# Sketched attention with a routed expert layer: two changes of order, the count of the first half moved ahead of its take, and a search and pick moved behind a copy

## The chip, the cores and the metric

The kernel runs on one core of a Trainium2 chip. A core has five engines that run side by side[...]: TensorE (PE, with its weight loads shown apart as PEld), VectorE (DVE), ScalarE (ACT), GpSimd (POOL) and SyncE (SP), which here issues most of the transfers. The metric is the device time of one execution in microseconds; less is better.

## What is computed

The first half is attention with a polynomial sketch, for q, k and v of 4 batches, 4 heads, 1088 rows and 32 columns. Its result, seen as 4352 rows (tokens) of 128, goes to a layer of 8 experts, of which each token uses one.

```python
def phi(x):                                   # 8 by 8 products of two sketches
    a = einsum('rd,bhsd->bhsr', S1, x); b = einsum('rd,bhsd->bhsr', S2, x)
    return einsum('bhsi,bhsj->bhsij', a, b).reshape(..., 64)
q_p, k_p = phi(q), phi(k)
kv, z = einsum('bhsf,bhsd->bhfd', k_p, v), k_p.sum(axis=2)
attn = einsum('bhsf,bhfd->bhsd', q_p, kv) / (einsum('bhsf,bhf->bhs', q_p, z)[..., None] + 1e-6)
x = attn.transpose(0, 2, 1, 3).reshape(4352, 128)

xn = x / (norm(x) + 1e-6); en = emb / (norm(emb) + 1e-6)
logits = xn @ en.T / tau
expert_idx = argmax(logits, axis=1)
probs = softmax(logits); gate_w = probs[arange(N), expert_idx]
for e in range(8):
    mask = expert_idx == e
    out[mask] = gate_w[mask, None] * (relu(x[mask] @ w1[e]) @ w2[e])
```

## The kernel before, in words

**Two halves of the tokens.** The four batches are worked in two halves (m = 0 and 1), each of two batches. For a half, the keys' features are made and multiplied with v (L479), and the queries' features give the numerators and denominators in PSUM (`nd`, L613). `x` (L626 to L633, on DVE) divides them and makes the rows `xg` and the scaled logits `lg`.

**The router.** For a stretch of columns of a half, `router` (L677) makes these steps. `best` (L683, L684) searches the largest logit and stores the distances into the row. `pick` (L690 to L695) makes the one-hot choice `oh` and its sum `total`. `place` (L703 to L707) adds up on TensorE, in PSUM, each token's place within its expert. `take` (L712, DVE) reads those sums out of PSUM with the one-hot choice, and `split` (L718 to L720) and `mark` (L727) prepare a product that inverts the list. `write` (L733, L737) sends the rows to DRAM through SP. Half 0 is one stretch; half 1 has two, columns 0 to 7 and 8 to 16.

**The count.** `count` in `plan_early` (L831) calls `tokens_by_expert` (L820): two small products on TensorE (L824, over `less` and the first half's `total`) and one rounding on DVE (L825), which gives the number of full blocks of each expert. The count of half 0 lies in the same PSUM tile as the placing (`spare[0]`), in other columns. `rest` (L835 to L839), `find` (L791, L795), `sums` (L800, L802) and `tokens` (L817) turn counts and places into the lists of rows of the first ten blocks, which the gathers (`fetch`, L930, on POOL) use.

**The blocks.** Tokens of one expert are gathered in blocks of 128 rows, counted from 0. For block i: `turn` (L936 on TensorE, and the copy L938, on ACT for blocks 0, 1 and 4 to 8, else on DVE), `up` (first layer, L984, and the rectifier L992 on ACT), `down` (second layer, L1020), and the scaled store (L1029, L1032). The gate needs `norm` (L997, L998), `inverse` (L1001), `shares` (L1008) and `share` (L1011, L1012). `weights` (L947, SP) loads the first layer's weights two blocks ahead.

**What sets the order.** The engines' instructions are in the order in which the steps are emitted. Two lists written by hand, `HEAD` and `ORDER`, hold the steps up to block 0. From then on there are ticks, one for each block (tick 10 is block 0), and within a tick the steps are sorted by a rank: `up` at 30, `turn` of the next block at 45, `share` at 73, `down` of the block before at 74, `norm` at 74.6. Steps of the second half's router are put in by pairs (tick, rank). Each engine takes its part of that order and works it off in sequence.

Of the kernel before, what the change touches and what calls it, by code (L numbers as in the profile page):

```python
# [65 lines left out]
def kernel(  # L66
# [25 lines left out]
    def ps_big():  # L92
        return psum.tile([P, 2, 512], F32, tag="big", bufs=2, name="ps_big")
# [159 lines left out]
    total = {(m, c): consts.tile([P, E], BF16, name=f"total{m}_{c}") for m in range(NM) for c, _ in SPANS[m]}  # L253
# [108 lines left out]
total0; ktr 1; ktr 3; tremb; kab 0 ab; trkv0; kvT0; kb 0; kab 1 acc; kp 0; ktr r; kve0; kz0; kb 1; kab 3 ab;  # L362
ktr 2; nd 0 0; kab 2 t; kab r ab; nd 0 1; x 0 0; kb 2; x 0 1; trqp0r; nd 0 2; kb 3; kp 1; kb r; kv 0; x 0 2;
nd 0 3; kp 2; x 0 3; qtr 1; kp 3; qtr 0; kv 2; qab 0 t; qb 0; qtr 3; kp r; best 0; kv 3; qtr r; qp 0; qtr 2;
place 0; take 0; count; kv 1; kv r; trqp 0; total; split 0; qab 1 t; trkv; qab 3 ab; rest; mark 00; qb 1;
qab r ab; mark 01; find; exp0; kvT; qab 2 acc; sums; kve; qb 2; qpT 0; qb 3; qb r; qp 1; tokens; qp 3; kz;
trqp 1; nd 1 0; fetch0; fetch 1; qp 2; x 1 0; qp r; trqp 3; qpT 1; others; qpT 3; nd 1 1; x 1 1; norm 0; turn 0; trqp 2;
qpT 2
# [154 lines left out]
    def queries(m, c0, c1, tick=None):  # L523
# [128 lines left out]
        if c1 == s1:  # L652

            bank = (lambda: spare[m]) if m == 0 else ps_small if c1 < NC else (lambda: table_bank[0][:, 0])
            best, pick, place, take, split, mark, write = router(m, s0, s1, g, bank)

            if m == 0:
                steps.update({"best 0": best, "pick 0": pick, "place 0": place, "take 0": take, "split 0": split,
                              "mark 00": lambda: mark(0, NK), "mark 01": lambda: mark(NK, NC), "write 0": write})
            elif c1 < NC:  # L660
                at_rank = {best: (10, 72), pick: (10, 72), write: (11, 80), place: (12, 31.5),
                           take: (12, 44), split: (13, 76.5), mark: (14, 76)}
            else:
                at_rank = {best: (12, 31), pick: (12, 31), place: (13, 31), take: (13, 32), split: (13, 32),
                           write: (12, 90), mark: (16, 32)}
                put_at(13)(0, 30.9, lambda: table_bank.append(ps_big()))
            if m == 1:
                for f, (t, rank) in at_rank.items():
                    put_at(t)(0, rank, f)
# [157 lines left out]
    def plan_early():  # L827

        full, upto, w = column("full"), column("upto0"), column("w_early")

        def count():  # L831
            tokens_by_expert((less,), full, spare[0][:, NC * E:(NC + 1) * E])

        def rest():
            nc.vector.tensor_tensor_scan(out=upto[:], data0=ones_e[:], data1=full[:], initial=0.0, op0=ALU.mult, op1=ALU.add)  # L835
            nc.vector.tensor_scalar(w, full, -1.0, float(KEYS), op0=ALU.mult, op1=ALU.add)
            first, early["expert_0"], early["experts"] = blocks(0, upto, w, lane)
            at = first()
            nc.vector.tensor_add(at, at, lane[:, :EARLY])  # L839
            early["key"] = at  # L840

        def others():
            nc.vector.tensor_scalar_min(c_early[:, 1:], upto, float(EARLY))
            early["took"] = column("took")
            nc.vector.tensor_sub(early["took"], c_early[:, 1:], c_early[:, :E])
        return count, rest, others
# [195 lines left out]
    def put_at(tick):  # L1042
        def put(after, rank, f):
            at.setdefault(tick + after, []).append((rank, len(at.get(tick + after, ())), f))
        put.tick = tick
        return put

    for i, group in enumerate(GROUPS):
        for tiles in group:
            for m in range(NM):  # L1050
                keys(m, *tiles, i)
                queries(m, *tiles, i)
# [5 lines left out]
    count, rest, others = plan_early()  # L1058
# [20 lines left out]
    count, rest, shared, others, experts = plan_late()  # L1079
# [100 lines left out]
```

## Time and profile before

| | |
|---|---|
| time, median of 3 runs | 205.55 us (205.15 to 206.97) |
| the profiled execution | 204.43 us |
| its span, first to last instruction | 202.6 us |
| instructions | 6949 |
| TensorE's granted clock | 1.000 |
| HBM read, written | 34.37 MB, 4.73 MB |

The page of the profile begins with busy time by engine and gives the chain of work that ended last. Further views are the waits (who stood still, and what released it), and the timeline: start in us, duration in us, engine, line, operation, `out<-in`, shapes and count, and in brackets the idle time before it with its releaser. A row with x16 is sixteen instructions merged. PE's rows are the products, PEld's the loads of their weights; ends of PE's rows are modelled.

### The profile page before, as it was taken

How to read it: one execution, taken by the hardware profiler on the slowest of the kernel's cores; microseconds unless marked ns; L12 is line 12 of the kernel's file. 1: busy time of each engine (PE TensorE's matmuls, PEld its weight loads, DVE VectorE, ACT ScalarE, POOL GpSimd, SP SyncE). 2: the span in 40 equal slices, each digit the busy share in tenths (PEclk: the TensorE clock that was granted, in tenths of full speed). 3: DMA queues.
4: the chain of work that ended last, by engine and by line, in shares of the span. 5: the costliest groups of instructions: out<-in, count | busy, mean ns of one | idle time of the engine just before them, and what ended most of it. 6: DMA issues, size and time to landing. Idle time of an engine off the chain costs nothing.

```text
span 202.6 us, 6949 instructions
## 1 busy us (share of the span) xinstructions
PE 192.7 (95%) x2586; PEld 182.7 (90%) x2586; DVE 87.6 (43%) x378; ACT 102.4 (51%) x293; POOL 107.0 (53%) x137
## 2 busy tenths in 40 slices
PE   7889999999799999999999999999999999999991
PEld 7667888889689999999999999999999999988991
DVE  6677848888658488912222212222122122112200
ACT  2657451436464456434655546545555465766540
POOL 4000335303813767755878777677676776664043
PEclk9999999999999999999999999999999999999999
DMA  4998799987284886544466665657646784485000
GB/s 132 323 217 287 179 320 293 280 282 208 54 321 139 278 310 211 165 132 145 148 205 189 170 205 155 209 166 163 222 147 184 223 306 169 136 263 190 3 26 25
DMA packets 28162, 39.42 MB, mean 195 GB/s; under 512 B 5738, under 2 KB 21366, under 8 KB 28130
## 3 DMA queue, kind: packets, MB, share of 16 engines
q1 hardware_dynamic: 25776, 34.23, 55.9%
q0 software_dynamic: 2304, 4.74, 7.5%
q8 instruction: 22, 0.36, 0.7%
q14 instruction: 10, 0.08, 0.1%
q10 hardware_dynamic: 50, 0.01, 0.0%
HBM read 34.37 MB, written 4.73 MB: 193 GB/s over the span
## 4 chain that ended last, share of the span: by engine, by line
PE 90%; DVE 4%; ACT 2%; issue 1%; DMA 1%; POOL 0%; POOLq 0%; DVEq 0%
PE ps_big L984 28%; PE ps_ab L1020 14%; PE ps_acc L1020 13%; PE ps_big L613 5%; PE ps_acc L479 4%; PE ps_big L989 4%; PE ps_t L382 3%; PE ps_t L936 2%; PE ps_ab L401 2%; PE ps_big L561 2%; PE ps_acc L1023 2%; PE ps_ab L1023 2%; PE ps_t L802 2%; ACT qpT L570 1%; PE ps_ab L591 1%
## 5 line engine op out<-in xcount | busy, mean ns | idle before, releaser
L984 PE MATMUL ps_big<-xTb,wb 128*128 128x128 f32 x512 | 63.0, 276 | 1.6 <-ACT xTb L938 1.4
L984 PEld LDWEIGHTS ps_big<-xTb,wb 128*128 128x128 f32 x512 | 59.7, 192 | 2.4 <-ACT xTb L938 1.6
L1032 POOL DMA_INDIRECT out_dram<-y,dst_i x36 | 37.7, 1048 | 42.9 <-ACT y L1029 24.4
L992 ACT ACTIVATE hT<-ps_big 128x1024 f32<-128x1024 f32 x36 | 36.9, 1024 | 41.3 <-issue 22.7
L930 POOL DMA_INDIRECT xs<-rows,dst_i x36 | 37.3, 1035 | 18.8 <-DVE dst_i L817 11.3
L938 DVE COPY xTb<-ps_t 128x128 f32<-128x128 f32 x29 | 8.4, 290 | 59.4 <-issue 38.2
L1020 PE MATMUL ps_ab<-w_sb,hT 128*128 x256 | 31.3, 275 | 0.0
L1020 PE MATMUL ps_acc<-w_sb,hT 128*128 x256 | 31.2, 275 | 0.0
L1020 PEld LDWEIGHTS ps_ab<-w_sb,hT 128*128 128x128 f32 x256 | 29.9, 192 | 0.0
L1020 PEld LDWEIGHTS ps_acc<-w_sb,hT 128*128 128x128 f32 x256 | 29.9, 192 | 0.0
L998 POOL TENSOR_TENSOR norm<-norm,half_c 128x1 f32<-128x1 f32 x36 | 21.6, 604 | 4.5 <-ACT sq L997 4.1
L1011 DVE TENSOR_SCALAR gate<-gate 128x1 f32<-128x1 f32 x36 | 5.5, 152 | 23.2 <-ACT probs L1008 16.4
L1029 ACT ACTIVATE y<-ps_ab,gate 128x128 f32<-128x128 f32 x17 | 6.2, 367 | 11.0 <-PE ps_ab L1020 6.4
L1029 ACT ACTIVATE y<-ps_acc,gate 128x128 f32<-128x128 f32 x18 | 6.6, 366 | 9.9 <-PE ps_acc L1020 6.8
L1008 ACT ACTIVATE probs<-xs,norm 128x8 f32<-128x8 f32 x36 | 10.6, 295 | 1.2 <-DVE norm L1001 1.2
L997 ACT ACTIVATE sq<-xs 128x128 f32<-128x128 f32 x36 | 10.8, 301 | 0.2
L936 PE MATMUL ps_t<-ident,xs 128*128 128x128 f32 x36 | 10.2, 282 | 0.2 <-issue 0.2
L417 POOL TENSOR_TENSOR kp<-both 128x1024 f32<-128x1024 f32 (+1 forms) x4 | 6.5, 1624 | 7.0 <-ACT both L412 4.8
L479 PE MATMUL ps_acc<-v,kp 128*64 128x64 f32 x256 | 9.2, 225 | 0.5 <-issue 0.5
L319 POOL TENSOR_TENSOR emb_ss<-emb_ss,half_c 8x1 f32<-8x1 f32 x1 | 0.6, 576 | 17.1 <-ACT emb_sq L318 17.1
L479 PEld LDWEIGHTS ps_acc<-v,kp 128*64 128x64 f32 x256 | 8.2, 138 | 1.5 <-issue 1.5
L989 PE MATMUL ps_big<-xTb,wb 128*64 128x64 f32 x128 | 8.3, 224 | 0.3 <-issue 0.2
(254 smaller groups left out, 293.7 us busy)
## 6 DMA issues: line engine op xcount, KB each, us to landing
wb<-in_moe_w_dram SPq DMA_DIRECT2D x36, 512.0 KB
w_sb<-in_moe_w_dram SPq DMA_DIRECT2D x16, 256.0 KB
rows<-xg SPq DMA_DIRECT2D x4, 544.0 KB
v<-in_v_dram SPq DMA_DIRECT2D x4, 512.0 KB
v<-in_moe_w_dram SPq DMA_DIRECT2D x4, 512.0 KB
k<-in_k_dram SPq DMA_DIRECT2D x3, 512.0 KB
q<-in_q_dram SPq DMA_DIRECT2D x3, 512.0 KB
xs<-rows,dst_i POOLq DMA_INDIRECT x36
```

The costliest lines, as they stand in the source:

```text
L479: nc.tensor.matmul(acc[m][u * HALF:(u + 1) * HALF, i, p], s["kp"][:, c - c0, h], bass.AP(tensor=vo.tensor, offset=vo.offset, ap=[list(vo.a ...
L930: nc.gpsimd.indirect_dma_start(out=xs[i][:], out_offset=None, in_=rows[:2 * S if t == 0 else N + 1], in_offset=bass.IndirectOffsetOnAxis(a ...
L936: nc.tensor.transpose(ps[:, :P], xs[i][:, :DM], ident)
L984: nc.tensor.matmul(ps[:, u, j * P:(j + 1) * P], w[:, f * P:(f + 1) * P], x, start=True, stop=True)
L989: nc.tensor.matmul(ps[r, u, j * P + b * HALF:j * P + (b + 1) * HALF], wh[:, f * P + c * HALF:f * P + (c + 1) * HALF], x[:, b * HALF:(b + 1 ...
L992: nc.scalar.activation(hT[i], ps, ACT.Relu)
L997: nc.scalar.activation(sq, xs[i][:, :DM], ACT.Square, accum_out=norms[i])
L998: nc.gpsimd.tensor_tensor(out=norms[i], in0=norms[i], in1=half_c, op=ALU.pow)
L1008: nc.scalar.activation(p, xs[i][:, DM:], ACT.Exp, scale=norms.pop(i)[:, 0:1], accum_out=gate[i])
L1020: nc.tensor.matmul(ps, h[:, f * P:(f + 1) * P], ws[0][:, f], start=f == 0, stop=f == NF - 1)
L1029: nc.scalar.activation(y, ps, ACT.Copy, scale=gate.pop(i)[:, 0:1])
L1032: d = nc.gpsimd.indirect_dma_start(out=out[:, :], out_offset=bass.IndirectOffsetOnAxis(ap=dst_i[t][:, j:j + 1], axis=0), in_=y[:], in_offs ...
```

## The change

Two places in the order change; no instruction is added, removed or altered in its operands.

In `ORDER`, `count` moves from behind `take 0` to ahead of it. TensorE's order stays as it was, since `take` has no product: the placing, then the count's two products. On DVE the rounding of the count (L825) now comes ahead of the take (L712).

For the first stretch of half 1, `best` and `pick` move from (10, 72) to (11, 45.1) and (11, 45.2). Tick 11 has `turn` of block 2 at rank 45, so they come right behind that block's copy of turned rows. Between the old and the new place on DVE lie `share` of block 0 (L1011, L1012) and the copy of block 2 (L938); these three now run first, and then the six operations of `best` and `pick`. The orders of TensorE, ACT, POOL and SP are the same as before.

```diff
@@ -362,7 +362,7 @@
-place 0; take 0; count; kv 1; kv r; trqp 0; total; split 0; qab 1 t; trkv; qab 3 ab; rest; mark 00; qb 1;
+place 0; count; take 0; kv 1; kv r; trqp 0; total; split 0; qab 1 t; trkv; qab 3 ab; rest; mark 00; qb 1;
@@ -658,7 +658,7 @@
             elif c1 < NC:
-                at_rank = {best: (10, 72), pick: (10, 72), write: (11, 80), place: (12, 31.5),
+                at_rank = {best: (11, 45.1), pick: (11, 45.2), write: (11, 80), place: (12, 31.5),
                            take: (12, 44), split: (13, 76.5), mark: (14, 76)}
```

## The prediction

> **What bounds the kernel now.** I read the share of busy time and the chain that ended last on the page, then TensorE's waits in the stretch of the two edits, then the timeline around each edit.
>
> ```profile
> PE 192.7 (95%) x2586; PEld 182.7 (90%) x2586; DVE 87.6 (43%) x378; ACT 102.4 (51%) x293; POOL 107.0 (53%) x137
> ...
> PE 90%; DVE 4%; ACT 2%; issue 1%; DMA 1%; POOL 0%; POOLq 0%; DVEq 0%
> ```
>
> TensorE is busy 95% of the span and makes 90% of the chain. A change of order on other engines can only win where TensorE stands still. Its waits from 40 to 80 us, complete (sum, times, longest):
>
> ```profile
> PE ps_big L984 <- ACT xTb L938: 1.4, 1, 1.4
> PE ps_big L824 <- DVE lt L712: 0.4, 1, 0.4
> PE ps_big L984 <- DVE norm L1001: 0.2, 1, 0.2
> ```
>
> The second and third are the places that the change touches; the first lies between them and is untouched. From 64.70 on a block takes 3.68 us on TensorE (L1020 starts at 71.32, 75.00, 78.69), with hardly a gap to the end, so what is won before 64.70 should reach the end and nothing more is to be had after it.
>
> First place (timeline: start, duration, engine, line, operation, idle before it and releaser):
>
> ```profile
> 41.46 0.10 PEld L824 LDWEIGHTS <-ones 128*128 128x128 bf16 x1
> 41.66 0.30 DVE L712 TENSOR_TENSOR lt<-ps_big,oh 128x136 f32<-128x136 f32 x1 [0.37 <-PE ps_big L707]
> 42.02 0.17 PE L824 MATMUL ps_big<-less,ones 128*128 128x8 bf16 x1 [0.39 <-DVE lt L712]
> 42.02 0.10 PEld L824 LDWEIGHTS <-ones 128*128 128x128 bf16 x1 [0.46 <-issue]
> ...
> 42.24 0.17 DVE L825 TENSOR_SCALAR full<-ps_big 128x8 f32<-128x8 f32 x1 [0.28 <-PE ps_big L824]
> 42.33 0.28 DVE L718 TENSOR_REDUCE mx<-lt 128x17 f32<-128x136 f32 x1
> ...
> 45.77 0.60 DVE L795 TENSOR_TENSOR hits<-hits,digits 128x180 bf16<-128x180 bf16 x2
> ...
> 46.61 1.20 DVE L417 TENSOR_TENSOR qp<-both 128x1024 f32<-128x1024 f32 x1
> ...
> 46.79 1.09 PEld L802 LDWEIGHTS <-row 128*128 128x128 bf16 x17
> ...
> 47.97 0.92 PEld L591 LDWEIGHTS ps_big<-ident,qp 128*128 128x128 f32 x8
> ```
>
> The counting product (L824) has its weights at 41.46 and runs at 42.02, when the take (L712) has read the same PSUM tile.
>
> Second place:
>
> ```profile
> 62.47 0.27 PE L936 MATMUL ps_t<-ident,xs 128*128 128x128 f32 x1
> ...
> 62.58 1.95 PE L1020 MATMUL ps_acc<-w_sb,hT 128*128 x16
> 62.66 0.21 DVE L683 TENSOR_REDUCE mx<-lg 128x8 f32<-128x64 f32 x1
> ...
> 64.12 0.14 DVE L1011 TENSOR_SCALAR gate<-gate 128x1 f32<-128x1 f32 x1
> ...
> 64.38 0.27 DVE L938 COPY xTb<-ps_t 128x128 f32<-128x128 f32 x1
> ...
> 64.70 1.86 PEld L984 LDWEIGHTS ps_big<-xTb,wb 128*128 128x128 f32 x16 [0.36 <-DVE norm L1001]
> ```
>
> Blocks are counted from 0. Block 2's rows are turned by 62.74, but their copy (L938) runs at 64.38, behind search and pick (L683 to L695). The first layer of block 2 (L984) follows at once.
>
> **What the Trainium skill says.** "Perfetto Trace Analysis", section "Tensor Engine Instruction (MATMUL, LD_WEIGHTS)": a matmul's start is observed, its end estimated. So I take gains from start to start, not from idle times; the trace fits, since L824's gap reads 0.39 on PE and 0.46 on PEld. "TensorE: Matmul & The Clock Gate", the table at its head: Vector and Scalar queues are strict FIFO. The trace agrees: L938 stood 1.64 us behind a transpose that was done. "PSUM — Partial Sum Buffer", section "PSUM bank collisions raise a hardware error": guard by bank and quadrant, not by address. That fits L824's 0.39 us wait on a read of other columns; no run here shows a collision.
>
> **First edit.** It adds and removes no instruction. On TensorE, ACT, POOL and SP the order stays; on DVE, L825 (0.17) goes ahead of L712 (0.30). The counting product no longer waits for a read; its second half waits for the count of the first pick, done at 40.16 (L695). The loads before it start at most (0.67 - 0.10)/15 = 0.04 apart, so the second load of L824 comes near 41.50 instead of 42.02: **0.52 us** for TensorE (by the page's idle 0.39, the other bound). What is late next is DVE. L825 must now wait for the counting product, whose estimated end is 41.50 + 0.17 = 41.67; it starts near 41.75. Short DVE operations follow each other 0.09 apart (42.24, 42.33), so the take runs from 41.84 to 42.14 and L718 at 42.17 instead of 42.33: DVE wins only 0.16. Behind that DVE is busy without a break up to 47.81 and TensorE needs two of its results. L802 needs the hits: ended at 46.37, now 46.21, against 46.79 - 0.52 = 46.27: just in time. L591 (47.97) needs qp, done at 47.81, now 47.65, and about 0.04 for the signal: it starts at 47.69 instead of 47.45. So TensorE keeps 47.97 - 47.69 = **0.28 us**. Behind it ACT's copies follow TensorE's products, with gaps of 0.98 and 0.92 ahead of L412 that move with TensorE, and the place where DVE writes the token lists (L817) waits for L802, so the gathers on POOL behind it come earlier, not later. SP's order and waits are untouched here. Bounds: 0.52 if DVE's results come earlier than I think, 0 if the next wait takes all. I take 0.28.
>
> **Second edit.** Six DVE operations (0.21, 0.22, 0.22, 0.22, 0.22, 0.27; 62.66 to 64.21 = 1.55 us) move behind L1011, L1012 and L938. Nothing is added or removed. The gate needs ACT's sums, done at 59.78, the copy the turned rows, done at 62.74; so gate at 62.66, its reciprocal at 62.84, the copy about 62.93 to 63.20, without a wait. L984 then starts when TensorE is through with L1020: 1.79 after its start, as in the next block (67.03 to 68.82), 62.58 + 1.79 = 64.37 instead of 64.70: **0.33 us**. Bounds: 0.17 (idle on PE) and 0.36 (idle on PEld). Queued behind the moved six on DVE are the norms (L1001, 64.57): the same nine operations stand ahead of them, so they, and ACT's L1008 at 64.94 which waits for them, keep their time. The pick ends near 64.75 instead of 64.21. Its readers: the placing L703, at 66.48 - 0.33 = 66.15, 1.4 us later; the write of rows on SP (63.16), which waits for L684, comes about 0.55 later, and with it the weights queued behind it on SP (64.12), the fifth block's. They are used at 76.79 - 3.68 = 73.11, 8.4 us after the later issue, while block 1's weights were issued at 54.07 and used at 60.58, within 6.5. The next SP write waits for the second search (65.88), which keeps its place. POOL's queue is passed by nothing. So these cost nothing; if that cover were gone it would be 0.55 at most.
>
> **The wait between them.** The 1.4 us at 55.26: TensorE's last start ahead of it is 53.26, yet ACT's copy for block 0 starts only at 54.94, and DVE too is held until 54.90, both by TensorE's signals. The page doesn't say why. If its end moves with TensorE, the 0.28 passes; if something at a fixed time ends it, the 0.28 is lost; if it closes, up to 1.4 more. I take the first, as nothing but TensorE released both engines.
>
> **Sum.** 0.28 + 0.33 = 0.61 us. The profiled execution took 204.43 us (202.6 of span and 1.8 around it): 203.8. The median of the runs shown is 205.55, 1.1 above it, so I forecast 205.55 - 0.6 = **204.9 us**, 0.3% less.
>
> **Rivals.** (a) The first edit's gain is swallowed, by qp on DVE or by the wait at 55.26, or the counting product still finds a wait: only 0.33 remains, 205.2. For it: DVE's short gain, a margin of 0.06 at L802. Against: L591 had 0.16 to spare. (b) The wait at 55.26 closes or shrinks, too: 204.9 - 1.4 = 203.5. For it only that its cause isn't shown. (c) Slower: search and pick end late and DVE passes it on. Behind them stand the second search, the take (67.27) and block 3's copy (L938, 67.41 to 67.69), which the first layer of block 3 needs at 68.71 - 0.61 = 68.10. The copy has moved by the 0.28 as well, so some 0.7 us is spare. DVE's work must be late by more than 0.7 + 0.61 = 1.3 us to make the kernel slower than before; it could come from the copy, which now holds the search back until TensorE has turned block 2's rows, if TensorE reaches that turn late (its weights landing late). For a delay of 2 us it gives 205.55 + 0.7 = 206.3. Against: the turn ends at 62.74, before DVE asks for it.
>
> **How the numbers follow.** Forecast 0.70, (a) 0.15, (b) 0.06, (c) 0.09. The three runs shown range from 205.15 to 206.97, so the median of a few is uncertain by some 0.5. Range: 204.9 less the rest of the first edit (0.24) and the scatter, 204.1, up to (a) with its scatter, 205.8. About 1% (2.06 us) is what can be told from no change; the sum is a third of that. Faster by over 1% needs nearly all of (b) with the sum: 0.05; slower by over 1% takes (c) at some 3.4 us: 0.04; within 1%: 0.91.
>
> **What would show it.** Right: no wait of L824 on L712; L825 ahead of L712 and L718 about 0.16 earlier; L591 behind qp with a gap near zero; L984 of block 2 1.8 us after L1020's start and no wait on DVE there; the span some 0.6 shorter, all of it before 65 us. Wrong: a new wait of TensorE on DVE between 42 and 48 or at L703 near 66, the gap at 55.26 changed by more than 0.3, or weights awaited near 73.

## The result, and the profile after

The changed kernel took **204.08 us** (median of 8 executions, 203.53 to 204.81) against 205.56 (204.94 to 206.97) for the kernel before: a ratio of 0.9923, interval [0.9893, 0.9952], so about 1.5 us less where 0.6 was forecast. Run twice more among the experiments, the same kernel gave 0.9942 [0.9917, 0.9967] and, on another chip, 0.9977 [0.9956, 0.9998]. Comparisons leave out executions over 1.5% above the fastest of their kernel, most of them at a lower granted clock (at most 4 for most kernels, but 9, 10 and 13 of 22 for gathers later, tensor extra and lists later, whose ratios look the better for it), and the profiles of pick only, tensor extra, lists later and last, extra are of such executions, so that I read from them only stretches ahead of or behind their loss of clock.

The profiled execution of the changed kernel has a span of 202.8 us, no shorter than the 202.6 of the kernel before. That says nothing about the change: the placing (L703), the last thing ahead of it, starts at 41.30 instead of 40.74, because this execution lost 0.56 us earlier. So from here on I count times in each trace **from the start of its first L703**.

The page of the changed kernel, busy shares and the chain that ended last:

```profile
PE 192.6 (95%) x2586; PEld 182.6 (90%) x2586; DVE 87.4 (43%) x378; ACT 102.4 (50%) x293; POOL 107.4 (53%) x137
...
PE 84%; DMA 5%; ACT 4%; DVE 3%; issue 2%; POOL 0%; POOLq 0%; ACTq 0%; DVEq 0%
```

TensorE is as busy as before (192.6 us). The new 5% for DMA has little to do with the change: 3.8% is the gather of a later block, from 71.23 to 78.88, and TensorE was busy throughout that stretch. TensorE's waits from 40 to 80 us, complete:

```profile
PE ps_t L936 <- issue: 1.6, 1, 1.6
```

The waits of L824 on L712 (0.4) and of block 2's L984 on DVE (0.2) are gone; the one ahead of block 0 is still there, now booked at the turn (L936). In this execution the other reader of block 0's gathered rows, L997 on ACT, stood as well and started with it (54.50 and 54.52), so both waited for the rows, and not for a copy as before. The timeline of the changed kernel at the three places (start, duration, engine, line, operation, idle before it and releaser):

```profile
42.04 0.17 PE L824 MATMUL ps_big<-less,ones 128*128 128x8 bf16 x1
...
42.28 0.17 DVE L825 TENSOR_SCALAR full<-ps_big 128x8 f32<-128x8 f32 x1 [1.39 <-PE ps_big L824]
42.36 0.29 DVE L712 TENSOR_TENSOR lt<-ps_big,oh 128x136 f32<-128x136 f32 x1
...
48.11 0.16 DVE L817 TENSOR_REDUCE dst_i<-ps_t 128x10 int32<-128x20 f32 x1
...
48.24 0.86 PEld L591 LDWEIGHTS ps_big<-ident,qp 128*128 128x128 f32 x8
...
53.32 0.94 POOL L930 DMA_INDIRECT xs<-rows,dst_i  x1 [0.30 <-issue]
...
54.50 0.31 ACT L997 ACTIVATE sq<-xs 128x128 f32<-128x128 f32 x1 [2.13 <-issue]
...
54.52 0.33 PE L936 MATMUL ps_t<-ident,xs 128*128 128x128 f32 x1 [1.59 <-issue]
...
54.94 0.17 DVE L626 TENSOR_SCALAR rc<-ps_big 128x16 f32<-128x16 f32 x1 [1.60 <-PE ps_t L936]
...
62.79 1.95 PE L1020 MATMUL ps_acc<-w_sb,hT 128*128 x16
...
63.13 0.27 DVE L938 COPY xTb<-ps_t 128x128 f32<-128x128 f32 x1
63.32 0.21 DVE L683 TENSOR_REDUCE mx<-lg 128x8 f32<-128x64 f32 x1
...
64.58 1.95 PE L984 MATMUL ps_big<-xTb,wb 128*128 128x128 f32 x16
```

Counted from L703, L824 runs at 0.74 (before 1.27), L825 now stands ahead of L712, the list of block rows (L817) is written at 6.81 (7.27), L591 loads at 6.94 (7.23). In the second place block 2's rows are copied at 63.13, ahead of the search (63.32), and L984 follows 1.79 after L1020 with no wait. Between the two lies the gap. In the kernel before, the list of block rows and the gap looked like this:

```profile
48.01 0.18 DVE L817 TENSOR_REDUCE dst_i<-ps_t 128x10 int32<-128x20 f32 x1 [0.20 <-PE ps_t L802]
...
53.30 0.94 POOL L930 DMA_INDIRECT xs<-rows,dst_i  x1 [0.30 <-issue]
...
54.90 0.17 DVE L626 TENSOR_SCALAR rc<-ps_big 128x16 f32<-128x16 f32 x1 [1.59 <-PE ps_ab L591]
54.94 0.27 ACT L938 COPY xTb<-ps_t 128x128 f32<-128x128 f32 x1 [2.48 <-PE ps_ab L591]
...
55.25 1.86 PEld L984 LDWEIGHTS ps_big<-xTb,wb 128*128 128x128 f32 x16 [1.63 <-ACT xTb L938]
```

TensorE had ended what L626 and L938 read by 53.0, yet both start at 54.9, 0.66 after the end of GpSimd's fourth gather (53.30 + 0.94 = 54.24).

### The profile page after: what moved, and what is told of

Same layout as the page of the kernel before. It is cut to its first block, busy times and chain, and to the rows that moved or that the text cites. A ratio compares the mean times of both kernels' runs of the same rounds, so it can differ in the third digit from the quotient of the medians.

```text
span 202.8 us, 6949 instructions
## 1 busy us (share of the span) xinstructions
PE 192.6 (95%) x2586; PEld 182.6 (90%) x2586; DVE 87.4 (43%) x378; ACT 102.4 (50%) x293; POOL 107.4 (53%) x137
## 4 chain that ended last, share of the span: by engine, by line
PE 84%; DMA 5%; ACT 4%; DVE 3%; issue 2%; POOL 0%; POOLq 0%; ACTq 0%; DVEq 0%
PE ps_big L984 27%; PE ps_ab L1020 13%; PE ps_acc L1020 12%; PE ps_big L989 4%; PE ps_acc L479 4%; PE ps_big L613 4%; DMA xs<-rows,dst_i 4%; PE ps_t L382 4%; PE ps_t L936 2%; PE ps_ab L401 2%; PE ps_big L561 2%; PE ps_acc L1023 2%; PE ps_ab L1023 2%; ACT qpT L570 1%; PE ps_t L802 1%
## 5 line engine op out<-in xcount | busy, mean ns | idle before, releaser
L984 PE MATMUL ps_big<-xTb,wb 128*128 128x128 f32 x512 | 62.9, 276 | 0.1
L984 PEld LDWEIGHTS ps_big<-xTb,wb 128*128 128x128 f32 x512 | 59.7, 192 | 0.7 <-ACT xTb L938 0.3
L1032 POOL DMA_INDIRECT out_dram<-y,dst_i x36 | 38.4, 1067 | 41.3 <-ACT y L1029 20.5
L930 POOL DMA_INDIRECT xs<-rows,dst_i x36 | 37.1, 1029 | 19.3 <-DVE dst_i L817 11.8
L938 DVE COPY xTb<-ps_t 128x128 f32<-128x128 f32 x29 | 8.4, 290 | 59.4 <-issue 38.2
L1020 PE MATMUL ps_ab<-w_sb,hT 128*128 x256 | 31.3, 275 | 0.0
L1020 PE MATMUL ps_acc<-w_sb,hT 128*128 x256 | 31.2, 275 | 0.0
L1020 PEld LDWEIGHTS ps_ab<-w_sb,hT 128*128 128x128 f32 x256 | 29.9, 192 | 0.0
L1020 PEld LDWEIGHTS ps_acc<-w_sb,hT 128*128 128x128 f32 x256 | 29.9, 192 | 0.0
L998 POOL TENSOR_TENSOR norm<-norm,half_c 128x1 f32<-128x1 f32 x36 | 21.6, 603 | 5.6 <-ACT sq L997 5.4
L1011 DVE TENSOR_SCALAR gate<-gate 128x1 f32<-128x1 f32 x36 | 5.4, 151 | 23.4 <-ACT probs L1008 17.5
L997 ACT ACTIVATE sq<-xs 128x128 f32<-128x128 f32 x36 | 10.9, 302 | 4.1 <-issue 2.1
L936 PE MATMUL ps_t<-ident,xs 128*128 128x128 f32 x36 | 10.2, 282 | 1.6 <-issue 1.6
```

The lines of the kernel that those rows point to most:

```text
L930: nc.gpsimd.indirect_dma_start(out=xs[i][:], out_offset=None, in_=rows[:2 * S if t == 0 else N + 1], in_offset=bass.IndirectOffsetOnAxis(a ...
L936: nc.tensor.transpose(ps[:, :P], xs[i][:, :DM], ident)
L984: nc.tensor.matmul(ps[:, u, j * P:(j + 1) * P], w[:, f * P:(f + 1) * P], x, start=True, stop=True)
L997: nc.scalar.activation(sq, xs[i][:, :DM], ACT.Square, accum_out=norms[i])
L998: nc.gpsimd.tensor_tensor(out=norms[i], in0=norms[i], in1=half_c, op=ALU.pow)
L1020: nc.tensor.matmul(ps, h[:, f * P:(f + 1) * P], ws[0][:, f], start=f == 0, stop=f == NF - 1)
```

## The experiments

The table gathers what the traces show, in us from the start of L703. "Gathers end" is the end of the run of gathers (L930) that GpSimd issues before block 0's norm (L998). L626 is the second batch's second group, DVE's first reader of a product of TensorE in the gap; L984 the first layer of a block. Empty fields lie behind a loss of clock.

| kernel | gathers in the run | gathers end | L626 | L984 block 0 | block 1 | block 2 |
|---|---|---|---|---|---|---|
| before | 4 | 13.50 | 14.16 | 14.51 | 19.84 | 23.96 |
| before again | 4 | 13.50 | 14.21 | 14.56 | 19.98 | 24.10 |
| pick only | 4 | 13.49 | 14.21 | 15.25 | | |
| count only | 4 | 12.97 | 13.66 | 14.13 | 19.36 | 23.49 |
| changed | 4 | 12.97 | 13.64 | 14.26 | 19.49 | 23.28 |
| changed again | 4 | 12.97 | 13.67 | 14.02 | 19.42 | 23.21 |
| changed, third | 4 | 12.97 | 11.96 | 14.13 | 19.35 | 23.14 |
| experts early | 4 | 12.96 | 13.63 | 14.13 | 20.22 | 24.00 |
| both moves | 1 | 8.56 | 11.88 | 14.19 | 21.75 | 25.50 |
| gathers later | 1 | 8.48 | 11.96 | 12.61 | 21.54 | 25.33 |
| gathers split | 2 | 10.47 | 11.96 | 12.61 | 18.43 | 22.22 |
| gather last | 3 | 11.71 | 12.19 | 12.61 | 17.96 | 21.75 |
| gather last again | 3 | 11.72 | 11.96 | 12.61 | 17.83 | 21.62 |
| last, no count | 3 | 12.25 | 12.50 | 12.95 | 18.18 | 21.96 |
| last, extra | 3 | 11.72 | 12.56 | 13.48 | 18.70 | 22.48 |
| lists later | 4 | 13.20 | 14.62 | 14.97 | | |
| tensor extra | 4 | 12.97 | 15.20 | 15.55 | | |

### The two edits apart, and both kernels again

Count only is the kernel before with the first of these edits, pick only with the second; the other two are the two kernels again.

```diff
-place 0; take 0; count; kv 1; kv r; trqp 0; total; split 0; qab 1 t; trkv; qab 3 ab; rest; mark 00; qb 1;
+place 0; count; take 0; kv 1; kv r; trqp 0; total; split 0; qab 1 t; trkv; qab 3 ab; rest; mark 00; qb 1;
...
-                at_rank = {best: (10, 72), pick: (10, 72), write: (11, 80), place: (12, 31.5),
+                at_rank = {best: (11, 45.1), pick: (11, 45.2), write: (11, 80), place: (12, 31.5),
```

> Only the first edit (count ahead of take). Theory 'two own gaps': the first edit is worth its gap of 0.3 to 0.5 us and no more, ratio about 0.998, no wait of TensorE on L712, the second gap (L984 of block 2, 0.36 on PEld) still there. Rival 'the wait ahead of block 0 carries it': the lists of rows come earlier, and with them the gather that block 0 waits for near 54 us, so this edit alone is worth 1.0 us or more, ratio 0.995 or less. Rival 'scatter': both edits together are worth 0.6 as forecast and this one 0.3.

> Only the second edit (first search and pick of the second half behind block 2's copy). Theory 'two own gaps': 0.33 us, ratio about 0.9985; L984 of block 2 starts 1.79 us after L1020 before it, the wait of L824 on L712 is still there. Rival 'the wait ahead of block 0 carries it': the same 0.33, since this edit lies behind block 0. If it is worth 0.8 or more, something behind 65 us moves that I did not see.

> The kernel before, unchanged, as a control: ratio 1.000 within 0.2%. Its profile shows how the gap of TensorE near 54 us (1.4 us in the first profile) and the gaps without a releaser (0.5 us at 33) differ from one execution to the next: 'scatter' expects them to differ by more than 0.5 us.

> The changed kernel, unchanged, as a second measurement: theory 'two own gaps' and 'the wait ahead of block 0' expect 0.992 to 0.994 again; 'scatter' expects 0.996 to 0.998. Its profile shows whether the wait of block 0's turn on its gather (1.6 us near 54) comes back.

Count only: 204.91 us, ratio 0.9958 [0.9930, 0.9986]. Pick only: 205.26, 0.9974 [0.9940, 1.0008], not to be told from no change. Before again: 0.9991 [0.9968, 1.0015]. Changed again: 204.34, 0.9942 [0.9917, 0.9967]. The times add up (0.9 and 0.5 to 1.2), but their intervals are too wide to separate 0.28 from 0.5. The table does it. Block 2 starts at 24.03 before (mean of two), 23.49 with the first edit, 23.21 with both (mean of three): 0.54 for the first edit and 0.28 more, against 0.28 and 0.33 in the forecast. Behind block 2 nothing is gained or lost: from there to the end the traces of these kernels take 137.9 to 138.2 us (136.8 on the chip of changed, third). The second edit's size is read more closely from L1020 to the next L984: 2.12 to 2.14 in the traces without it, 1.78 or 1.79 in all with it, pick only among them (66.06 to 67.85, at full clock), where the wait of L824 (0.4) stays. The first edit's surplus arises at the gap, where L626 comes 0.5 us earlier while TensorE's own work ahead of it (L613 of that group) comes 0.35 earlier. Single executions scatter at block 0 itself (it starts at 14.5 twice, but at 15.25 in pick only, where nothing ahead of it was changed); L626 is steadier: 14.16 to 14.21 in all three traces without the first edit, 13.64 to 13.67 in three of the four of count only and the changed kernel. In the trace of changed again:

```profile
52.37 0.33 PE L936 MATMUL ps_t<-ident,xs 128*128 128x128 f32 x1
...
52.83 0.94 POOL L930 DMA_INDIRECT xs<-rows,dst_i  x1 [0.30 <-issue]
...
54.47 0.17 DVE L626 TENSOR_SCALAR rc<-ps_big 128x16 f32<-128x16 f32 x1 [1.63 <-PE ps_ab L591]
```

Block 0's turn ran at 52.37 here and at 54.52 in the first profile of the same kernel, 11.57 and 13.22 from L703, and yet L626 started at 13.67 and 13.64. So it isn't the turn that ends the hold. The end of the gathers, 12.97 in both, is the nearest thing that they share. (Where the next expectations count 4.9 us "after POOL's fourth gather", the distance is that from the start of the second gather, 9.26 to 14.16 before; from the start of the fourth it is 1.6.)

### Is it the gathers?

Gathers later moves the gathers of blocks 1 to 3 behind block 0's norm:

```diff
-trqp 1; nd 1 0; fetch0; fetch 1; qp 2; x 1 0; qp r; trqp 3; qpT 1; others; qpT 3; nd 1 1; x 1 1; norm 0; turn 0; trqp 2;
+trqp 1; nd 1 0; fetch0; qp 2; x 1 0; qp r; trqp 3; qpT 1; others; qpT 3; nd 1 1; x 1 1; norm 0; fetch 1; turn 0; trqp 2;
```

Experts early leaves the gathers alone and computes the experts' numbers (L769) right behind the first block's, so that the next weights are issued earlier; both moves does both.

```diff
-qab r ab; mark 01; find; exp0; kvT; qab 2 acc; sums; kve; qb 2; qpT 0; qb 3; qb r; qp 1; tokens; qp 3; kz;
+qab r ab; mark 01; find; exp0; experts0; kvT; qab 2 acc; sums; kve; qb 2; qpT 0; qb 3; qb r; qp 1; tokens; qp 3; kz;
...
-                  "others": together(others, lambda: early["experts"]()), "turn 0": lambda: turn(0), "norm 0": lambda: norm(0)})
+                  "others": others, "experts0": lambda: early["experts"](), "turn 0": lambda: turn(0), "norm 0": lambda: norm(0)})
```

> On the changed kernel, the gathers of blocks 1 to 3 are issued behind the norm of block 0, not right behind the gather of block 0; POOL's queue alone changes. In six profiles DVE's x of the second group (L626 near 54 us) starts 4.86 to 4.95 us after POOL's fourth gather, whatever TensorE does. Theory 'gathers hold it': then this start moves forward, and block 0's first layer comes about 1 us earlier, ratio to before near 0.989. Rival 'experts and weights hold it': the start stays 1.75 to 1.80 us behind L769, ratio as for the changed kernel, 0.993 to 0.994, or worse if block 1's rows then come late.

> On the changed kernel, the list of experts (L769) is written right behind the first expert (L766) near 47 us, so that SP issues the weights of blocks 1 to 3 some 5 us earlier; DVE's chain grows there by about 0.1 us and loses as much later. Theory 'experts and weights hold it': the start of L626 near 54 us moves forward with L769, block 0 comes about 1 us earlier. Rival 'gathers hold it': it stays 4.9 us behind POOL's fourth gather, time as for the changed kernel (0.993 to 0.994) or slower by up to 1 us, since 1.5 MB of weights then share the DMA engines with the gather of block 0.

> On the changed kernel, both moves: gathers of blocks 1 to 3 behind the norm of block 0, and experts early. If each holds the start by itself, only this one moves it; if one of them alone does, this is like that one. If neither matters, the wait of 1.6 us on DVE stays and the time is that of the changed kernel.

The timeline of gathers later:

```profile
52.77 0.15 DVE L626 TENSOR_SCALAR rc<-ps_big 128x16 f32<-128x16 f32 x1
...
53.11 1.00 POOL L930 DMA_INDIRECT xs<-rows,dst_i  x1 [0.18 <-issue]
...
57.31 0.33 PE L936 MATMUL ps_t<-ident,xs 128*128 128x128 f32 x1 [1.95 <-DMA xs<-rows,dst_i]
```

The gap ahead of block 0 is gone (L626 at 11.96 instead of 13.65), but block 1's gather now starts at 53.11, and TensorE waits 1.95 us for its rows. Timed: 0.9979 [0.9949, 1.0009], no gain over the changed kernel, and its block 2 starts 2.1 us later. Experts early did not free L626 (13.63): 0.9963 [0.9936, 0.9989]. It moved the weights ahead of the rows. TensorE's waits in it, complete:

```profile
PE ps_t L936 <- DMA xs<-rows,dst_i: 2.0, 2, 1.4
```

Both moves joined the two losses: 1.0077 [1.0049, 1.0105]. In its trace L626 is free, but block 0's rows come late:

```profile
53.77 0.17 DVE L626 TENSOR_SCALAR rc<-ps_big 128x16 f32<-128x16 f32 x1
...
55.04 0.33 PE L936 MATMUL ps_t<-ident,xs 128*128 128x128 f32 x1 [1.43 <-DMA xs<-rows,dst_i]
```

So the hold of L626 goes with the gathers and not with the expert numbers or weights. For block 0's start that is not enough: with a single gather in the run, but the weights issued early, it was 14.19, as late as in the changed kernel.

Three more runs varied the number of gathers in the run, and when they come. Gathers split keeps block 1's with block 0's and moves two behind the norm; gather last moves only block 3's (with `range(1, 2)` and `range(2, AHEAD)` the first edit below is that of gathers split). Lists later keeps all four and writes the row list four times, the last edit alone.

```diff
-trqp 1; nd 1 0; fetch0; fetch 1; qp 2; x 1 0; qp r; trqp 3; qpT 1; others; qpT 3; nd 1 1; x 1 1; norm 0; turn 0; trqp 2;
+trqp 1; nd 1 0; fetch0; fetch 1; qp 2; x 1 0; qp r; trqp 3; qpT 1; others; qpT 3; nd 1 1; x 1 1; norm 0; fetch 2; turn 0; trqp 2;
...
-"fetch 1": lambda: [fetch(i) for i in range(1, AHEAD)],
+"fetch 1": lambda: [fetch(i) for i in range(1, 3)], "fetch 2": lambda: [fetch(i) for i in range(3, AHEAD)],
```

```diff
-"tokens": lambda f=tokens: f(0, EARLY),
+"tokens": lambda f=tokens: [f(0, EARLY) for _ in range(4)],
```

> On the changed kernel, block 1's gather stays right behind block 0's, and the gathers of blocks 2 and 3 go behind block 0's norm on GpSimd. If the second group's release (L626) is tied to the end of GpSimd's run of gathers, it comes at about 12.0 us after the placing (L703) instead of 13.65, block 0's first layer at about 12.7 instead of 14.0 to 14.3, and, other than with all three gathers moved, block 1's rows are there in time (its first layer at about 18 instead of 19.4): the run is about 1 us faster than the changed kernel, 203.3 us. If block 0's rows or its expert weights set that release, L626 stays at 13.65 and the time is that of the changed kernel, 204.3. If the later gathers only push the wait on to block 2, its first layer comes as late as before and the time is the same too, with L626 early.

> On the changed kernel, only the gather of block 3 goes behind block 0's norm on GpSimd; those of blocks 1 and 2 stay. If the release is tied to the end of the run of gathers, L626 comes one gather (about 1.2 us) earlier than in the changed kernel, at about 12.4 us after the placing, between the changed kernel and the run with two gathers moved, and the time lies between theirs, at about 203.6. If the release is tied to anything else (the fourth gather's own rows, block 0's rows), it stays at 13.65 and the time at 204.3.

> On the changed kernel, VectorE makes the row list of the first table (L817) four times, so that GpSimd's gathers start about 0.65 us later, while the transposes of the third and fourth groups and the numerators on TensorE stay where they are (their own waits leave about that much room). If block 0's start hangs on the lists by way of the gathers, L626 and block 0's first layer come about 0.65 us later and the run takes about 205.0 us. If it hangs on TensorE's row of work, as the prediction had it, nothing ahead of block 0 moves and the time stays at 204.3.

Gathers split: 202.82 us, 0.9900 [0.9868, 0.9932]. Gather last: 202.63, 0.9900 [0.9871, 0.9929]. In both, block 0 starts at 12.61, 1.4 to 1.65 earlier than in the changed kernel, and block 1's rows are in time. Gather last:

```profile
50.84 0.94 POOL L930 DMA_INDIRECT xs<-rows,dst_i  x1 [0.30 <-issue]
...
52.26 0.17 DVE L626 TENSOR_SCALAR rc<-ps_big 128x16 f32<-128x16 f32 x1
52.29 0.27 ACT L938 COPY xTb<-ps_t 128x128 f32<-128x128 f32 x1 [0.81 <-PE ps_t L936]
```

The third gather ends at 51.78, and both readers of TensorE start 0.48 and 0.51 later. Lists later is the counter-test:

```profile
52.38 0.33 PE L936 MATMUL ps_t<-ident,xs 128*128 128x128 f32 x1
...
53.07 0.94 POOL L930 DMA_INDIRECT xs<-rows,dst_i  x1 [0.30 <-issue]
...
54.79 0.99 POOL L930 DMA_INDIRECT xs<-rows,dst_i  x1 [0.18 <-issue]
55.43 0.17 DVE L626 TENSOR_SCALAR rc<-ps_big 128x16 f32<-128x16 f32 x1 [2.09 <-remote]
...
55.78 3.38 PE L984 MATMUL ps_big<-xTb,wb 128*128 128x128 f32 x16 [2.20 <-issue]
```

Here TensorE's work ahead of the gap stands exactly where it did (turn at 11.57 from L703, as in changed again), the gathers start 0.24 (the fourth) to 0.64 us later, and L626 comes 0.97 later: 14.62. Had the gap's end moved only with TensorE, L626 would have stayed. Timed 1.0009 [0.998, 1.0038], above all three ratios of the changed kernel (0.9923 to 0.9977), though its interval meets that of the third. So the row list has its own way to block 0. That it leads by GpSimd is the likely reading and not shown by this run alone: the three extra operations also put DVE's own work back by 0.48 (L769 at 12.38 instead of 11.89), though DVE then stood idle for 2.09 us ahead of L626. The size fits less well: the fourth gather ends only 0.23 later, and L626 comes 1.42 behind it, inside the fifth, so a fixed distance of 0.5 to 0.7 is no law.

### Extra work on TensorE, with and without the gap

Tensor extra makes the eight transposes of the fourth group twice (L591, `c0 == 12`), on the changed kernel; last extra does so on gather last; last, no count undoes the first edit on gather last.

```diff
-            for p in range(2):
+            for p in (0, 1, 0, 1) if c0 == 12 else (0, 1):
```

> On the changed kernel, eight transposes (L591 of the fourth group, near 50.5 us) are made twice, with the same result: 0.88 us more of TensorE's work between the two edits' places. The prediction's view that the gap ahead of block 0 moves with TensorE expects block 0 and the end 0.88 us later. The rival, that its end is set by the lists of rows and what hangs on them, expects block 0 where it was, within 0.1 us, and the gap smaller by 0.88.

> The changed kernel once more, on the same chip as the three runs beside it: a ratio of 0.993 to 0.994 to the kernel before (0.9923 and 0.9942 so far), and the gap ahead of block 0's first layer in its trace (L626 at 13.65 us after the placing, block 0 at 14.0 to 14.3).

> The changed kernel with block 3's gather behind block 0's norm, once more: the gap ahead of block 0 gone, block 0's first layer at 12.6 us after the placing, and a ratio of 0.990 or lower to the kernel before; if the gap was the whole difference to the changed kernel, 1.4 us less than that kernel on the same chip, a ratio between the two of 0.993.

> As last_again, with the first edit undone (the count behind the take). With the gap gone, the edit should be worth what TensorE keeps of it, 0.28 to 0.35 us: block 0's first layer at 12.9 to 13.0 us after the placing and a time 0.3 to 0.4 us above last_again. If the edit's worth of half a microsecond and more comes from the row lists in any arrangement, block 0 comes 0.5 us later than in last_again and the time is 0.5 to 0.9 us above it.

> As last_again, with the eight transposes of the fourth group (L591) made twice, 0.88 us more on TensorE. In the changed kernel that cost about 1.7 us. If the surplus came from slipping behind GpSimd's gathers, it costs 0.9 us here: block 0's first layer at 13.5 us after the placing and a time 0.9 us above last_again. If TensorE's work in this stage costs double in any arrangement, the time is 1.7 us above it.

Tensor extra: 206.63 us, 1.0019 [0.9988, 1.005]; its L626 slipped by 1.55, behind a fifth gather (13.75 to 14.74), for 0.87 of work, with the gathers of the run unmoved. So TensorE is not without a say.

The last four ran on one chip, where the kernel before took 202.72 us (medians of all executions, means of those compared):

| kernel | median, us | ratio to before | mean of the executions, us |
|---|---|---|---|
| changed, third | 202.32 | 0.9977 [0.9956, 0.9998] | 202.21 |
| gather last again | 201.49 | 0.9952 [0.9931, 0.9973] | 201.48 |
| last, no count | 202.05 | 0.9956 [0.9934, 0.9979] | 201.97 |
| last, extra | 203.40 | 1.0019 [0.9996, 1.0041] | 203.11 |

Without the gap the first edit moves block 0 by 0.34 (12.95 to 12.61), what the forecast gave TensorE. TensorE's waits in last, no count show the edit undone, and nothing else:

```profile
PE ps_big L824 <- DVE lt L712: 0.4, 1, 0.4
```

In time that is 0.49 us by the means, with 0.46 either way (from standard deviations of 0.70 over 19 and 0.77 over 21 executions), and only 0.1 by the ratios: it agrees with 0.34 and can't measure it. Last, extra was to tell whether extra work is dearer because of the gap. The traces say yes (without the gap blocks 0 to 2 move by 0.86 or 0.87, against 1.3 to 1.5 for block 0 with it), the times don't: 1.63 by the means (0.47 either way), some 1.4 by the ratios, for 0.87 of work. That stays open.

The third trace of the changed kernel has another variant of the gap:

```profile
53.42 0.15 DVE L626 TENSOR_SCALAR rc<-ps_big 128x16 f32<-128x16 f32 x1
53.49 0.94 POOL L930 DMA_INDIRECT xs<-rows,dst_i  x1 [0.31 <-issue]
...
54.55 0.33 PE L936 MATMUL ps_t<-ident,xs 128*128 128x128 f32 x1 [1.45 <-DMA xs<-rows,dst_i]
```

L626 isn't held at all; instead block 0's rows are there only at 54.55, 0.12 after the fourth gather's end (53.49 + 0.94 = 54.43), and TensorE waits 1.45 for them. The expectation had L626 at 13.65 and missed; block 0 starts at 14.13 all the same. Two different signals are late in these traces, sometimes one, sometimes both, and with four gathers in a row block 0 never started before 14.0, with three or fewer and the weights' order unchanged always at 12.6 to 13.5.

**A version that beats both**, by the means, is gather last. On the same chip its mean is 0.73 us under the changed kernel's, with 0.42 either way (standard deviations 0.70 and 0.66, 19 and 21 executions), or 0.4%; by the ratios (0.9952 and 0.9977) it is 0.5, with overlapping intervals, and the 0.990 that was expected on this chip was missed. Its traces promise more: block 2 starts 1.52 earlier than in the changed kernel's trace from that chip, and all of it reaches the end (spans of 199.9 and 201.4 us). So the missing half isn't lost later in the kernel; the executions that weren't profiled differ by less than the two that were, perhaps by a smaller gap, which isn't shown.

## Why the prediction was wrong

**The count, L824.** Right: 0.53 earlier (forecast 0.52), the wait on L712 gone, L825 ahead of L712.

**DVE takes part of it back.** Right: L718 0.20 earlier (forecast 0.16); L591's loads 0.29 and L613 behind them 0.35 earlier (forecast 0.28). L802 still found its hits in time.

**The second edit.** Right: 0.33, L984 1.79 after L1020. The later rows and weights on SyncE cost nothing that the trace shows; TensorE has no wait on them up to 80 us.

**The wait between them** is the step that failed: "If its end moves with TensorE, the 0.28 passes; [...] I take the first, as nothing but TensorE released both engines." In the traces the gap's end moved not with TensorE's work (0.35 earlier) but with GpSimd's gathers. They hang on the row list (L817), which hangs on L802, and that product had kept nearly all of the count's gain: L817 moved by 0.46 and the fourth gather's end by 0.53. Where L626 was held it came 0.50 to 0.55 earlier, blocks 1 and 2 followed by as much (block 0 itself by 0.4), and the first edit was worth some 0.5 us at this place, not 0.28. The list was in the prediction's own sentence ("so the gathers on POOL behind it come earlier, not later"), booked as no harm; it was a gain. The mechanism of both edits was right; the term of the first was mis-sized, by a path that I had priced at nothing.

**The sum** is then 0.5 + 0.33 = 0.83 us, and block 2 starts 0.82 earlier in the traces (24.03 to 23.21). That would have given 204.7, so the mis-sized term accounts for only 0.2 of the 0.9 us by which the 1.5 exceeds the forecast. The three comparisons weighted by their intervals give 0.9953, about 1.0 us, with 0.0014 either way if they measured one and the same gain: in line with 0.83. The 1.5 us of the first comparison lies above that; its interval and that of the third (0.45 us by the means) don't overlap, so the gain differs between chips or occasions by more than each interval says. What made up the rest of the 1.5 no trace shows, and it stays open. Right was that what is won ahead of 64.70 us reaches the end, and that nothing is won behind it.

**The rivals.** (a), the gain swallowed, was wrong. (b), that the gap closes too (203.5), was wrong as well: it stayed, and only its end came 0.5 earlier. (c) did not occur: DVE's search and pick, 0.55 later, held nothing up.

What holds the signals or the rows while the gathers are being issued is not shown. The runs say that it goes when gathers are taken out of the run, that a later list delays it, and that late work of TensorE can be held longer still.

## What to carry to other kernels

Before a stall is booked as "moves with the engine that releases it", look for what its end coincides with on the other engines, in two executions if there are two: here the same turn ran 1.65 us apart in two traces and the stall ended at the same distance from a gather. An operation moved earlier should be followed along every reader, also those that seem only to gain. And a run of gathers issued ahead of need can cost more than it hides: issuing the last one behind the first block's norm gained some 0.7 us (0.4 either way), about as much as both edits on the path.

## What the runs showed of the hardware

- While GpSimd issued four indirect gathers in a row (0.94 to 1.75 us each), TensorE's results, or the landing of the first gather, reached their readers up to 2 us late: in the kernel before, L938 started at 54.94, 1.95 us after the end of the transpose that it reads (an end that is modelled). With three gathers in the run the delay was 0.3 us or none. The landing of the first gather was late in both moves too, with one gather in the run.
- A stall of TensorE well under 3 us was followed by a lower clock. In four traces it stood still for 1.91 to 2.20 us near block 0 (tensor extra 1.91, gathers later 1.95, pick only 2.10, lists later 2.20), and the clock granted from 56 to 60 us was 0.57 to 0.84. In the eight traces with a stall of 1.25 to 1.59 us there (the changed kernel's 1.59 the longest) it was 1.00. In lists later block 0's first layer took 3.38 us instead of 1.95 to 2.05, in tensor extra 2.97. The windows (stretch, its length, busy time of each engine, TensorE's granted clock, DMA share, GB/s) of lists later and of the changed kernel:

```profile
56.00:60.00 4.00, 4.00 (x31) 3.67 (x32) 1.41 (x5) 1.88 (x3) 0.00 (x0) 0.57 0.98 374
```

```profile
56.00:60.00 4.00, 4.00 (x71) 3.57 (x71) 1.90 (x8) 2.31 (x7) 0.74 (x1) 1.00 0.94 361
```

  The Trainium skill ("TensorE: Matmul & The Clock Gate", section "What's actually happening") has the clock fall to half after at least one idle window of some 3.4 us. The half agrees: in lists later the clock was 0.50 from 57 to 59 us and 1.00 again from 60 on. The length doesn't: the idle time ahead of it was 2.20, and in last, extra 1.72 us of idling at 186 us was followed by 0.50 from 189 to 191.
